# First chunk of the first expert in whole float32, batch 0 turned by transposes, and filler matmuls in TensorE's pauses

## The chip, the cores and the metric

One core of a Trainium2 chip runs the kernel. The metric is the time of an execution on the device in microseconds. Before the change three runs took 937.07, 938.40 and 940.15 us, so the median is 938.4 us.

## What is computed

An attention with two parts, a pooled one over means of four tokens and a local one over the nearest tokens, feeds two feed-forward layers, one after the other, for 2304 tokens of width 512.

```python
def _attn_ref(q, k, v):                      # 4 batches, 8 heads, 576 tokens, 64 wide
    q_d, k_d, v_d = (t.reshape(B, H, S // 4, 4, D).mean(axis=3) for t in (q, k, v))
    out_up = np.repeat(sm_attn(q_d, k_d, v_d), 4, axis=2)       # softmax attention, pooled
    mask = np.abs(pos[:, None] - pos[None, :]) < 4              # local attention
    scores = np.where(mask, scale * q @ k.T, -1e9)
    return out_up + softmax(scores) @ v
x = attention output as [2304, 512]
h = x @ w_in; x = np.where(h > 0, h, exp(min(h, 0)) - 1) @ w_out          # d_ff 2048
g = x @ w_gate; out = (g * sigmoid(g) * (x @ w_val)) @ w_o2               # d_ff 1536
```

The two weights of the first layer and the three of the second come as 64-bit floats; the kernel makes 32-bit floats of their bit patterns.

## The kernel before

**The planner.** The whole kernel is a list of tasks. `add(engine, cost, due, fn, reads, writes, ...)` records one; `Work.run` then plays the time out, with the costs that are written beside each task, and emits in each engine's program whatever ready task has the smallest due time. So the order of the instructions on each engine is settled ahead, and on the chip each engine runs its list in order and waits for what each entry needs. The capital names (`START`, `EAGER`, `PARTS`, ...) are due times and offsets of that list. `urge` gives everything that the first product needs a due time from the length of its chain. DMAs are issued from one queue, SP's. `fetched` models the loading of TensorE's own instructions, in blocks of 256; only some tasks state their number (`words`).

**Batch 0.** `add_first_batch` loads q and k in 16 DMAs, two heads and half the sequence each, 72 partitions with pieces of 1 KB, and turns each part by eight matmuls against `ident` (L734) into `qT` and `kT`; a copier (L352 on ACT, L354 on DVE) brings the result from its PSUM bank. `add_sums` pools four tokens (L620 on DVE, L625 and L626 on POOL). `add_pooled` does one pair of heads of the pooled attention: scores (L812), maxima (L819), exponentials (L825), weights (L835), their turning (L850), values (L866). `add_local` does one unit of 96 tokens of the local attention: scores (L640), softmax (L658 to L680), the spread into `bd` (L352), values (L709). Units 0 to 2 are the first chunk; units 3 to 5 come later, between its products. `add_split` adds both parts into `f` (L987), rounds the sum into `x[..., 0]` (L352 or L354) and puts the remainder in `x[..., 1]` (L998, POOL).

**Weights.** `add_weights` loads each block of 512 KB and makes words of it: `size` (L509, ACT), `rest` (L515 on ACT or L513 on DVE), `words` (L519, DVE). `add_weight_split` rounds a block (L352 or L356) and subtracts (L554, POOL), since the products are made of rounded parts, hi x hi, hi x lo and lo x hi, in `products` (L1010 to L1012).

**The first layer.** Chunks of 288 tokens run over 16 blocks f of the hidden width: `gemm1` (x to h), ELU on ACT and DVE, `gemm2` (g to the accumulators). `add_whole` does this for chunk 0. There gemm1 is twelve split products and needs the split of block ("in", f) and of x; gemm2 is already four plain float32 matmuls (L1044) with the unsplit block ("out", f). Chunks 1 to 4 use split blocks for both. The rest of the first layer and the second layer use a seven-product scheme.

**Start.** Seven bf16 matmuls of 512 columns (`warm_up`, L1692) run first; `clear` sets all of `qT` and `kT` to zero on POOL (L1696).

## Time and profile before

| | |
|---|---|
| median of three runs | 938.4 us |
| the profiled execution | 937.54 us |
| its span, from the first to the last instruction | 935.8 us |
| mean granted TensorE clock | 0.978 |
| TensorE busy | 913.0 us |
| DVE, ACT, POOL busy | 566.3, 523.1, 533.6 us |

The profile is one execution, recorded on the chip. Its views are the page with busy times, the busy time in chosen stretches, the engines' instructions in order of time, the groups of instructions by line, and the chain of waits that leads to the end. The granted clock is a share of full speed: 1.00 is 2.4 GHz, 0.50 is 1.2 GHz. A float32 matmul stands as two instructions; the record of a matmul is longer than the distance to the next one, as they overlap.

### The profile page before, as it was taken

To read this page: it belongs to the slowest core of one execution; us is meant where nothing else is said; L and a number is where in the kernel's file an instruction comes from. 1 tells how busy PE (TensorE), PEld (TensorE's weight loads), DVE (VectorE), ACT (ScalarE), POOL (GpSimd) and SP (SyncE) were. 2 spreads that over 40 slices of the span, in tenths; PEclk is the share of its full clock that TensorE was granted. 3 is DMA by queue.
4 is the path that set the end of the run, shared out by engine and by line. 5 is a ranking of instruction groups with operands and counts; after the bars stand their busy time and mean duration, and the time that the engine had idled before them with its cause. 6 is when DMAs were issued, how large, how long until landed. Compare 5 with 4: busy or idle time off the path is not lost.

```text
span 935.8 us, 19972 instructions
## 1 busy us (share of the span) xinstructions
PE 913.0 (98%) x7573; PEld 829.0 (89%) x7573; DVE 566.3 (61%) x937; ACT 523.1 (56%) x1125; POOL 533.6 (57%) x609
## 2 busy tenths in 40 slices
PE   8779999999999999999999999999999999999998
PEld 7568889999999999999999888887888887999998
DVE  2988777777677249444337385435434247896773
ACT  3988566454556457675665456555546435453441
POOL 6797956664665459489791408998899940000000
PEclk7589999999999999999999999999999999999999
DMA  6999445659745654565588613452554299854331
GB/s 172 309 270 276 82 125 126 139 178 315 132 114 152 189 186 140 163 204 195 187 296 326 247 61 124 169 191 91 210 181 183 104 350 308 273 170 135 127 113 46
DMA packets 194704, 172.12 MB, mean 184 GB/s; under 512 B 96176, under 2 KB 166192, under 8 KB 194608
## 3 DMA queue, kind: packets, MB, share of 16 engines
q1 hardware_dynamic: 194464, 170.58, 58.2%
q8 instruction: 60, 0.98, 0.4%
q14 instruction: 36, 0.29, 0.1%
q10 hardware_dynamic: 144, 0.26, 0.1%
HBM read 111.62 MB, written 59.18 MB: 183 GB/s over the span
## 4 chain that ended last, share of the span: by engine, by line
PE 91%; DMA 4%; DVE 2%; SPq 1%; ACT 1%; issue 1%; POOL 0%; DVEq 0%
PE bank L1010 28%; PE bank L1011 27%; PE bank L1012 27%; PE bank L1044 3%; PE bank L640 2%; PE bank L709 2%; DMA w<-in_v_dram 2%; DMA w<-in_moe_w_in_dram 1%; DMA w<-in_k_dram 1%; PE bank L915 1%; PE bank L909 1%; PE bank L962 1%; DVE xh L1191 1%; SPq L595 0%; DMA wd<-mid 0%
## 5 line engine op out<-in xcount | busy, mean ns | idle before, releaser
L1010 PE MATMUL bank<-xs,wu 128*128 128x512 f32 x336 | 133.4, 397 | 2.4 <-DVE blk L1223 2.0
L1012 PE MATMUL bank<-xs,wu 128*128 128x512 f32 x336 | 133.2, 396 | 0.0
L1011 PE MATMUL bank<-xs,wu 128*128 128x512 f32 x336 | 133.2, 396 | 0.0
L1010 PE MATMUL bank<-os,ys 128*128 128x256 f32 x378 | 107.2, 283 | 1.0 <-DVE o L1223 1.0
L1011 PE MATMUL bank<-os,ys 128*128 128x256 f32 x378 | 107.0, 283 | 0.0
L1012 PE MATMUL bank<-os,ys 128*128 128x256 f32 x378 | 106.9, 283 | 0.0
L1010 PE MATMUL bank<-x,w 128*128 128x288 f32 x320 | 100.2, 313 | 1.4 <-DVE e L1088 0.9
L1010 PE MATMUL bank<-g,w 128*128 128x288 f32 (+1 forms) x320 | 101.0, 316 | 0.0
L1223 DVE TENSOR_TENSOR blk<-bank,blk 128x512 f32<-128x512 f32 x72 | 49.5, 690 | 81.7 <-PE bank L1012 75.4
L1011 PE MATMUL bank<-g,w 128*128 128x288 f32 (+1 forms) x320 | 98.5, 308 | 0.0
L1012 PE MATMUL bank<-g,w 128*128 128x288 f32 (+1 forms) x320 | 98.3, 307 | 0.0
L1011 PE MATMUL bank<-x,w 128*128 128x288 f32 x320 | 95.3, 298 | 0.0
L1012 PE MATMUL bank<-x,w 128*128 128x288 f32 x320 | 94.9, 296 | 0.0
L1095 POOL TENSOR_TENSOR g<-e,g 128x288 fp32r<-128x288 f32 x64 | 57.2, 894 | 56.0 <-ACT g L352 44.7
L1220 ACT COPY blk<-bank 128x512 f32<-128x512 f32 x72 | 42.0, 585 | 72.9 <-PE bank L1012 66.0
L1010 PEld LDWEIGHTS bank<-xs,wu 128*128 128x128 f32 x336 | 63.3, 188 | 17.7 <-DVE blk L1223 2.9
L1012 PEld LDWEIGHTS bank<-xs,wu 128*128 128x128 f32 x336 | 63.3, 188 | 15.4
L1011 PEld LDWEIGHTS bank<-xs,wu 128*128 128x128 f32 x336 | 63.3, 188 | 14.0
L1010 PEld LDWEIGHTS bank<-os,ys 128*128 128x128 f32 x378 | 72.5, 192 | 1.6 <-DVE o L1223 1.4
L1011 PEld LDWEIGHTS bank<-os,ys 128*128 128x128 f32 x378 | 72.5, 192 | 0.1
L1012 PEld LDWEIGHTS bank<-os,ys 128*128 128x128 f32 x378 | 72.5, 192 | 0.0
L1191 POOL TENSOR_TENSOR wu<-s,wu 128x256 fp32r<-128x256 f32 x79 | 59.7, 783 | 18.5 <-ACT wu L1194 18.4
(213 smaller groups left out, 2525.3 us busy)
## 6 DMA issues: line engine op xcount, KB each, us to landing
yr<-yd SPq DMA_DIRECT2D x27, 512.0 KB
yd<-blk SPq DMA_DIRECT2D x24, 512.0 KB
os<-od SPq DMA_DIRECT2D x42, 256.0 KB
w<-in_moe_w_in_dram SPq DMA_DIRECT2D x16, 512.0 KB
w<-in_moe_w_out_dram SPq DMA_DIRECT2D x16, 512.0 KB
wp<-w SPq DMA_DIRECT2D x16, 512.0 KB
wu<-wp SPq DMA_DIRECT2D x16, 512.0 KB
u<-wd SPq DMA_DIRECT2D x32, 256.0 KB
```

The costliest lines, as they stand in the source:

```text
L640: nc.tensor.matmul(sc[j].t[s * QB:(s + 1) * QB, (u * NP + p) * QB:(u * NP + p + 1) * QB], parts["qT"][p].t[j * D:(j + 1) * D, a:a + QB], p ...
L709: nc.tensor.matmul(pvs[u].t[j * D:(j + 1) * D, p * U:(p + 1) * U], tvs[u].t[:, (2 * p + j) * D:(2 * p + j + 1) * D], bd.t[:, u, j * NP + p ...
L909: nc.tensor.matmul(sc[0].t[j * D:(j + 1) * D, 2 * G:3 * G], vs0.t[:, w, j], prT0.t[:, j, w], start=(w == 0), stop=(w == 1))
L915: nc.tensor.matmul(sc[j].t[:HALF, u * G:(u + 1) * G], t[:, 0, p, u * HALF:(u + 1) * HALF], t[:, 1, p], start=True, stop=True)
L1010: nc.tensor.matmul(ps, sh, mh, start=first, stop=False, skip_group_check=more)
L1011: nc.tensor.matmul(ps, sh, ml, start=False, stop=False, skip_group_check=more)
L1012: nc.tensor.matmul(ps, sl, mh, start=False, stop=last, skip_group_check=more)
L1044: nc.tensor.matmul(acc[0][i].t[:, :T1], wo.t[:, i * P:(i + 1) * P].bitcast(F32), ge(), start=f == 0, stop=f == NF1 - 1)
L1095: add("pool", 0.86, due - URGENT, lambda e=e, g=g: nc.gpsimd.tensor_tensor(out=g.t[:, 1], in0=e.t, in1=g.t[:, 0], op=ALU.subtract), reads= ...
L1191: return task(engines, n, due, lambda engine=engines[0]: two(engine).tensor_tensor(out=out(), in0=in0(), in1=in1(), op=op), reads, writes, ...
L1220: return add("act", ps_copy, when(m) - 20, lambda: nc.scalar.copy(d(i), ps.t[:, :w]), reads=[ps], writes=of(i))
L1223: return add("dve", ps_sum, when(m) - 20, lambda: nc.vector.tensor_tensor(out=d(i), in0=ps.t[:, :w], in1=d(i), op=ALU.add), reads=[ps], wr ...
```

## The change

- Chunk 0: gemm1 becomes four plain float32 matmuls on the unsplit block ("in", f) and on x as it is. `add_split` writes the sum into x directly for this chunk. The splits of ("in", f) are made later, for chunk 1, rounded by ACT alone, as those of ("out", f).
- Batch 0: q and k are loaded as eight parts of two heads with the whole sequence, six tokens to a partition, 96 partitions, two DMAs with pieces of 256 bytes each. Each part is turned by six transposes of 96 x 128 (both heads at once) into two banks. The rows of v for the pooled part come in one load for two, and token pairs are interleaved in the matmuls' access patterns. Local scores wait for all parts.
- TensorE's pauses: where the planner finds TensorE without a ready task, from the first turning to the first product, it emits a bf16 matmul that nobody reads, 32 x 64 or 128 x 512. The warm-up becomes 72 of the small ones. Bank 7 is kept for it.
- Every task of TensorE states or estimates its number of instructions; `fetched` uses it for all.
- `clear` covers only the margins. The value loads are tasks by piece, with their memsets apart. `add_weights` may put raw blocks in any slot once products run; `add_direct` uses a PSUM bank. ACT may scale the pooled weights. Most due times and several costs have new values.

```diff
         t.costs = {engine: cost} if isinstance(engine, str) else dict(zip(engine, cost))
+        t.words = words + 1 if words else int(self.RATE * t.costs.get("pe", 0.0)) + 1
...
                     if t is None:
+                        filled = engine == "pe" and self.filler and self.filler()
+                        if filled:
+                            free[engine] = now + self.fetched(2, now, filled)
+                            seq += 1
+                            heapq.heappush(events, (free[engine], seq, None))
...
-                    if t.words:
-                        cost = self.fetched(t, now, cost)
+                    if engine == "pe":
+                        cost = self.fetched(t.words, now, cost)
...
-        return banks.new(lambda: [4, 5] if late or begun else [6, 0, 1, 2, 3, 7])
+        return banks.new(lambda: [4, 5] if late or begun else [6, 0, 1, 2, 3])
...
-    WARM = 7
+    WARM = 72
+    SHORT = 435.62
...
-            raw, w, ps = w_raws.new(lambda: range(NW - 1, U1 - 1, -1)), whole(n), bank(4, 5)
+            raw, w, ps = w_raws.new(lambda: range(NW - 1, -1 if begun else U1 - 1, -1)), whole(n), bank(4, 5)
...
-        for k, (p, u, which) in enumerate((p, u, which) for p in range(NP) for u in range(2) for which in range(2)):
+        for k, (p, which) in enumerate((p, which) for p in range(NP) for which in range(2)):
             name, start = (("qT", 0), ("kT", PAD))[which]
-            t, dst, pt = rows[k], parts[name][p], att_bank()
-            cols = slice(start + u * UPC * U, start + (u + 1) * UPC * U)
-            add("sp", 0.5, FIRST + 0.5 * k, lambda t=t, p=p, u=u, name=name: nc.sync.dma_start(
-                out=t.t, in_=rows_of(name[0], 0, u, 2 * p, 2 * p + 2)), writes=[t], nbytes=HALF * 2048 * 1.2)
-
-            def turn(t=t, pt=pt):
-                for r in range(R):
...
-            add("pe", 0.56, FIRST + k - EAGER, turn, reads=[t], writes=[pt, dst], slack=SLACK, kind="small", after=ready[:1], words=32)
-            made[which, p, u] = add(COPIER, (0.41, 0.45), FIRST + k + 1, lambda engine, dst=dst, pt=pt, cols=cols: copy(
-                engine, dst.t[:, cols], pt.t[:, :UPC * U]), reads=[pt], writes=[dst], second=1)
+            t, dst = rows[k], parts[name][p]
+            full = dst.room.make(p)[:, start:start + S]
+
+            def load(t=t, p=p, name=name):
+                for j in range(2):
+                    nc.sync.dma_start(
+                        out=t.t.rearrange("g (r j d) -> g r j d", j=2, d=D)[:, :, j],
+                        in_=source[name[0]][0, 2 * p + j].rearrange("(g r) d -> g r d", r=SIX))
+
+            add("sp", 1.0, FIRST + 1.0 * k, load, writes=[t], nbytes=P * S * 4 * 1.35)
+            of = []
+            for u in range(2):
+                pt, to = att_bank(), full.rearrange("c (g r) -> c r g", r=SIX)[:, 3 * u:3 * u + 3]
+
+                def turn(t=t, pt=pt, u=u):
+                    turning.append(1)
+                    for r in range(3):
+                        nc.tensor.transpose(
+                            pt.t[:, r * S // SIX:(r + 1) * S // SIX], t.t[:, (3 * u + r) * P:(3 * u + r + 1) * P], ident[:S // SIX, :S // SIX])
+
+                add("pe", 0.3, FIRST + 2 * k + u - EAGER, turn, reads=[t], writes=[pt, dst], slack=SLACK, kind="small", after=ready[:1], words=6)
+                of.append(add(COPIER, (0.41, 0.46), FIRST + 2 * k + u + 1, lambda engine, to=to, pt=pt: copy(
+                    engine, to, pt.t[:, :S // 2].rearrange("c (r g) -> c r g", r=3)), reads=[pt], writes=[dst], second=1))
+            made[which, p] = of
             summed.setdefault((0, p), []).append(add_sums(
-                FIRST + k + 2, lambda dst=dst, cols=cols: dst.t[:, cols].rearrange("p (g r) -> p g r", r=R),
...
-        for u in range(2):
-            t = raws[u]
-            add("sp", 0.5, load_due, lambda u=u, t=t: nc.sync.dma_start(
-                out=t.t, in_=rows_of("v", b, u, 2 * p, 2 * p + 2)), writes=[t], nbytes=HALF * 2048 * 1.2)
-            rowed.append(add("pool", 1.18, due, lambda t=t: add_rows(t.t), reads=[t]))
...
+        add("sp", 0.5, load_due, lambda: nc.sync.dma_start(
+            out=raw.t, in_=rows8("v", b, 2 * p, 2 * p + 2)), writes=[raw], nbytes=HALF * 4096 * 1.15)
+        rowed.append(add("pool", 2.05, due, add_rows, reads=[raw]))
...
                     nc.tensor.matmul(
-                        sc[j].t[:HALF, u * G:(u + 1) * G], t[:, 0, p, u * HALF:(u + 1) * HALF], t[:, 1, p], start=True, stop=True)
-
-        add("pe", 0.9, due + 1 - EAGER, scores, words=16, holds=[qk], after=summed[b, p], writes=[*sc, mx, nm, su, pr], slack=SLACK, kind="small")
+                        sc[j].t[:HALF, u * G:(u + 1) * G], t[:, 0, p].rearrange("c (g u) -> c g u", u=2)[:, :, u], t[:, 1, p], start=True, stop=True)
...
         add("dve", 1.35, due + 2 - FREE, maxima, reads=sc, writes=[mx, nm])
         add("act", 1.14, due + 3 - FREE, weigh, reads=[*sc, nm], writes=[pr, su])
         add("dve", 0.6, due + 4, norm, reads=[su], writes=[su])
-        add(EITHER, (1.01, 1.14), due + 4.3, weight, reads=[pr, su], writes=[pr])
+        add(("act", *EITHER), (1.28, 1.01, 1.14), due + 4.3, weight, reads=[pr, su], writes=[pr], second=1)
...
-                            pws[j].t[:HALF, w * G + u * HALF:w * G + (u + 1) * HALF],
-                            pr.t[:, j, u, w * HALF:(w + 1) * HALF], ident[:HALF, :HALF])
+                            pws[j].t[:HALF, w * G:(w + 1) * G].rearrange("k (g u) -> k g u", u=2)[:, :, u],
+                            pr.t[:, j, u].rearrange("q (k w) -> q k w", w=2)[:, :, w], ident[:HALF, :HALF])
...
-        add(EITHER, (0.77, 1.05) if n >= UPC else (1.0, 0.9), due, lambda engine: both(engine, f()), reads=[xf, xdT[b]], writes=[xf])
+        if c == 0:
+            return add(EITHER, (1.0, 0.9), due, lambda engine: both(engine, x.t[:, :, 0, cols].bitcast(F32)), reads=[xf, xdT[b]], writes=[x])
+        add(EITHER, (0.77, 1.05), due, lambda engine: both(engine, f()), reads=[xf, xdT[b]], writes=[xf])
...
-        add_weight_split(("in", f), due - EARLY, w_slots.new(lambda: range(NW)), ("pool", "act"), PREFER)
-        wi, wo, x = wt["in", f], ww["out", f], xt[0]
+        wi, wo, x = ww["in", f], ww["out", f], xt[0]
...
-                cs = slice(i * P, (i + 1) * P)
-                products(h.t[:, :T1], (wi.t[:, 0, cs], wi.t[:, 1, cs]), (x.t[:, i, 0], x.t[:, i, 1]), i == 0, i == NP - 1)
+                nc.tensor.matmul(
+                    h.t[:, :T1], wi.t[:, i * P:(i + 1) * P].bitcast(F32), x.t[:, i, 0].bitcast(F32), start=i == 0, stop=i == NP - 1)
...
-        inner[:] = [add("pe", 12 * 0.1325, due - STEP, gemm1, reads=[wi, x], writes=[h], after=inner)]
+        inner[:] = [add("pe", 1.73, due - STEP, gemm1, words=16, reads=[wi, x], writes=[h], after=inner)]
...
-        last[0] = [add("pe", 1.93, due + STEP, gemm2, reads=[wo, g], writes=acc[0], after=last.get(0, ()), slack=1.0)]
-        split_last = [add_weight_split(("out", f), time1(NF1 + f + 1) + PARTS, w_slots.new(split_places), COPIER[:1])]
+        last[0] = [add("pe", 1.73, due + STEP, gemm2, words=16, reads=[wo, g], writes=acc[0], after=last.get(0, ()), slack=1.0)]
+        split_last = [add_weight_split(("in", f), time1(NF1 + f) + PARTSI, w_slots.new(split_places), COPIER[:1]),
+                      add_weight_split(("out", f), time1(NF1 + f + 1) + PARTS, w_slots.new(split_places), COPIER[:1])]
...
-        raw = gens.new([P, 1024], I32, name="r")
+        raw, ps = gens.new([P, 1024], I32, name="r"), banks.new(lambda: range(8) if ending else range(4, 8))
...
         def warm_up():
             for _ in range(WARM):
-                nc.tensor.matmul(warm, zeros[:, :P], zeros, start=True, stop=True)
+                nc.tensor.matmul(warm[:QB, :64], zeros[:, :QB], zeros[:, :64], start=True, stop=True)
+
+        def fill():
+            if begun or not turning:
+                return 0.0
+            if work.words < SHORT and (work.border - work.words > 16 or work.arrives < work.now):
+                nc.tensor.matmul(warm[:QB, :64], ident.bitcast(BF16)[:, :QB], ident.bitcast(BF16)[:, :64], start=True, stop=True)
+                return work.FILLS[1]
+            some = ident.bitcast(BF16).rearrange("p (o n) -> p o n", o=1).to_broadcast([P, 2, 2 * P])
+            nc.tensor.matmul(warm.rearrange("p (o n) -> p o n", o=2), ident.bitcast(BF16)[:, :P], some, start=True, stop=True)
+            return work.FILLS[0]
+
...
         def clear():
-            for name in ("qT", "kT"):
-                nc.gpsimd.memset(turned[name], 0.0)
...
+            nc.gpsimd.memset(q[:, :, S:], 0.0)
+            nc.gpsimd.memset(k[:, :, :PAD], 0.0)
+            nc.gpsimd.memset(k[:, :, PAD + S:], 0.0)
...
-            add("sp", 2.0, LATER + n if late else VALUES + n, lambda n=n: load_values(0, n * U, vals[n].t), writes=[vals[n]], nbytes=P * H * D * 4 * 3.1)
-            turned_by = [t for (which, p, u), t in made.items() if u == (late or 0) or (which and (n == UPC - 1 or n == UPC))]
+            for s, edge, load in value_pieces(0, n * U):
+                due = (LATER if late else VALUES) + n
+                clean = [add("pool", 0.52, -900.0 + s, lambda n=n, s=s: nc.gpsimd.memset(vals[n].t[s * QB:(s + 1) * QB], 0.0), writes=[vals[n]])] if edge else ()
+                add("sp", 0.5, due, lambda n=n, load=load: load(vals[n].t), writes=[vals[n]], after=clean, nbytes=QB * H * D * 4 * 1.8)
+            turned_by = [t for ts in made.values() for t in ts]
...
-        whole = [w_slots.new(lambda: range(U1)) for _ in range(NF1)]
...
+        whole = [w_slots.new(lambda: range(NW if begun else U1)) for _ in range(NF1)]
...
```

## Rows read from the trace of the kernel before

**Rows 1.** The page: busy us (share of the span) and instructions by engine.

```profile
PE 913.0 (98%) x7573; PEld 829.0 (89%) x7573; DVE 566.3 (61%) x937; ACT 523.1 (56%) x1125; POOL 533.6 (57%) x609
```

**Rows 2.** Busy time by stage: stretch, length, engines, granted clock, DMA share, GB/s.

```profile
32.00:46.00 14.00, 12.82 (x112) 11.18 (x112) 13.35 (x32) 13.32 (x33) 8.54 (x11) 0.51 1.08 355
...
52.60:56.00 3.40, 3.40 (x15) 3.18 (x14) 2.54 (x6) 2.26 (x4) 3.40 (x4) 0.51 1.07 219
...
60.00:124.00 64.00, 63.84 (x598) 54.04 (x598) 51.99 (x101) 43.87 (x96) 50.94 (x55) 1.00 0.78 195
124.00:936.00 812.00, 803.45 (x6308) 735.97 (x6294) 475.17 (x745) 439.15 (x922) 438.69 (x489) 1.00 0.55 179
```

**Rows 3.** The chain of waits, 0 to 130 us: start, us, what.

```profile
9.70 5.50 DMA w<-in_k_dram
```

**Rows 4.** TensorE in order of time: start, us, line, tiles, count, [idle before].

```profile
1.19 3.17 PE L1692 MATMUL warm<-bd 128*128 128x512 bf16 x7 [1.19 <-DVE bd L1687]
...
6.15 13.05 PE L734 MATMUL bank<-ident,w 72*64 72x72 f32 x224 [0.47 <-DMA w<-in_q_dram]
...
24.41 0.91 PE L812 MATMUL bank<-sums 64*72 64x144 f32 x8 [1.70 <-DVE w L658]
...
32.08 1.17 PE L850 MATMUL bank<-ident,w 72*72 72x72 f32 x8 [3.38 <-POOL w L835]
...
42.31 3.24 PE L709 MATMUL bank<-bd,w 128*64 128x96 f32 x32
...
52.56 0.61 PE L1010 MATMUL bank<-x,w 128*128 128x288 f32 x1
```

**Rows 5.** ACT, DVE and POOL in order of time, before the first product.

```profile
39.90 1.45 ACT L352 COPY bd<-w 32x192 f32<-32x192 f32 x4
...
46.61 0.47 ACT L352 COPY f<-bank 128x384 f32<-128x384 f32 x1
...
46.96 0.54 DVE L987 TENSOR_TENSOR f<-f,xdT 128x384 f32<-128x384 f32 x1
...
48.33 0.98 POOL L987 TENSOR_TENSOR f<-f,xdT 128x384 f32<-128x384 f32 x1
```

**Rows 6.** The chain of waits at clock 1.00: start, us, what, count.

```profile
70.94 0.76 PE bank L640 x49
...
75.45 0.13 PE bank L1010
...
77.04 1.94 PE bank L1044 x8
...
82.50 1.47 PE bank L709 x32
...
126.51 0.50 PE bank L962 x8
...
130.26 0.65 PE bank L909 x8
```

**Rows 7.** Groups by line from 20 to 53 us: count | busy, mean ns | idle.

```profile
L825 ACT ACTIVATE w<-bank,nm 72x144 f32<-72x144 f32 x16 | 5.8, 373 | 1.8 <-DVE nm L820 1.8
...
L835 POOL TENSOR_TENSOR w<-w,su 72x576 f32<-72x576 f32 x3 | 3.4, 1138 | 0.0
...
L819 DVE TENSOR_REDUCE mx<-bank 72x2 f32<-72x288 f32 x8 | 3.3, 443 | 0.5 <-PE bank L812 0.5
```

**Rows 8.** Busy time of four short stretches, columns as in rows 2.

```profile
4.00:12.00 8.00, 7.44 (x141) 6.77 (x142) 0.45 (x1) 3.19 (x8) 2.22 (x5) 0.76 0.80 205
...
10.00:12.00 2.00, 2.00 (x38) 2.00 (x36) 0.00 (x0) 0.84 (x3) 0.00 (x0) 0.50 0.86 208
...
22.00:24.00 2.00, 0.71 (x66) 0.60 (x64) 1.97 (x6) 0.52 (x2) 1.84 (x5) 1.00 0.39 86
...
90.00:96.00 6.00, 6.00 (x41) 5.58 (x40) 4.82 (x9) 5.12 (x12) 5.26 (x6) 1.00 0.95 136
```

**Rows 9.** Groups by line from 53 to 125 us, the rounding of weights on ACT.

```profile
L352 ACT CAST w<-w 128x512 fp32r<-128x512 f32 x15 | 8.8, 615 | 4.7 <-POOL w L554 2.5 <-POOL half L625 1.5 <-PE bank L1044 0.6
```

211 lines of the change are left out of this document (115 added, 96 removed).

## The prediction, made before the changed kernel was run

> **What bounds the kernel now.** Three views, in this order. First the page's busy times: TensorE is busy 913.0 of 935.8 us, apart from its own weight loading nothing is above 61%, so only two things can shorten this kernel: less TensorE work, or less time in which TensorE idles or runs at its lower clock [rows 1]. Second the busy time by stage: from 124 us to the end TensorE idles 8.55 us of 812, from 60 to 124 us 0.16 of 64, and the granted clock is 1.00, the 2.4 GHz level [rows 2]. Nearly all the rest lies before 56 us, where the clock is about 0.51, the 1.2 GHz level, in the rows of 32 to 46 and of 52.6 to 56 us [rows 2]. So the question is when the first chunk's products begin (52.56 us, [rows 4]) and what TensorE must do from there. After that moment the kernel is a queue of TensorE work: a microsecond earlier is a microsecond off the end, and a microsecond of added TensorE work comes straight on top.
>
> Third the start itself, in order of time. The last q/k load is issued at 9.70 us and lands at 15.2 [rows 3]. TensorE turns these rows into qT and kT without a pause from 6.15 to 19.20, 224 small matmuls at 58 ns each [rows 4] at a clock of 0.50 [rows 8]. The softmax of four pooled heads and three local units follows; from 32.08 to 45.55 us TensorE works through 112 instructions (32 turn the pooled weights, 32 are pooled values, 48 local values) at 0.51 [rows 2, 4]. Then x is finished: the last local output is copied at 47.08, added to the pooled part by 49.31, then rounded and its remainder subtracted, and the first product starts at 52.56 [rows 4, 5].
>
> **The change, part by part.**
>
> *x whole.* The sum now goes straight into x; the copy and the remainder fall away for three units. After the copy at 47.08 there is one addition: 0.54 us on DVE, 0.98 on POOL [rows 5]. x is ready at 47.6 to 48.1 where the first product started at 52.56: 4.5 to 5.0 us, of which I take 4.5.
>
> *Products of the first chunk in float32.* The second product of this chunk has that form already: four matmuls, eight instructions, 1.94 us. The first one takes from 75.45 to 77.04, that is 1.59 us for twelve [rows 6]. It becomes 1.94, so 16 x 0.35 = 5.6 us are added, in a stretch where TensorE idles 0.16 us of 64 [rows 2]. Nothing covers that: it counts whole.
>
> *Splits of the input weights behind.* They no longer stand before the first product, but the first split was done before x was, so I take nothing for it beyond the first part. All 32 roundings go to ACT now, which made 15 of them from 53 to 125 us [rows 9], the others mostly POOL. That is a debt, below.
>
> *Turning by transposes.* 256 instructions become 48 transposes of 96 columns. Eight transposes of 72 columns take 0.50 us at clock 1.00 [rows 6] and 1.17 at 0.5 [rows 4], so one of 96 takes 83 to 195 ns, and only the last six (0.5 to 1.2 us) can lie behind the last landing, instead of 4.0 us. Against it, q and k come in pieces of 256 bytes instead of 1 KB. Pieces of 1 KB ran at 205 GB/s with the DMA engines 0.80 busy, 256 GB/s per full share; the v loads with pieces of 256 bytes at 86 with 0.39, 220 per full share; pieces of 128 bytes at 136 with 0.95, 143 [rows 8]. 2.36 MB at a share of 0.80 thus take 11.5, 13.4 or 20.7 us: 0 to 9.2 us more. I take 1.9, the row with the same size of piece. The turning then ends at 17.6 to 18.3 instead of 19.2; I take 1.2 us.
>
> The Trainium skill ("DMA: Bandwidth & Descriptors", Why small descriptors are slow) gives a descriptor of 256 bytes 11 bus cycles where 8 move data. By that an estimate for these loads is 11.5 x (11/8)/(35/32) = 14.5 us, 3.0 more than now instead of my 1.9; its specifications call for 512 bytes or more, which speaks against this part of the change.
>
> *Pooled heads during the loads.* TensorE had no room for pooled scores before 19.2 us. With the turning cheaper it has, and heads 0 to 2 can run while later heads still load. Per head ACT spends 4 x 0.37 us, DVE 2 x 0.44, POOL 1.14 [rows 7]; three heads are up to 4.4 us on ACT, which is busy 13.32 of 14 us from 32 to 46 [rows 2]. Bounds 0 and 4.4; I take 3, as ACT was nearly full there. The local scores wait longer instead: for all eight parts, not for one half. Behind them on TensorE stand the pooled scores, whose parts come earlier, so I add nothing.
>
> *Pauses filled.* If the clock is up from 32 us on, the 112 instructions take 4 x 0.50 (turning), 4 x 0.65 (pooled values), 1.5 x 1.47 (local values) = 6.8 us [rows 6] instead of 13.5. But ACT releases the last local values only at 41.35 [rows 5]; from there 0.7 (their matmuls) and 0.47 (the copy) lead to 42.5, not 47.08: 4.6 us. I take 4, between 0 and 6.7. Also the first products ran at half speed: 15 in 3.40 us [rows 2], which take 15 x 0.13 = 2.0 at 1.00 [rows 6], so 1.4 us more after the start. A filler in front of a ready instruction delays it by at most its own length; the seven matmuls of the warm-up, of the same form, took 3.17 us [rows 4], 0.45 each. The two long pauses, 1.70 us before 24.41 and 3.38 before 32.08 [rows 4], end in work of the chain: 0 to 0.9 us, I take 0.5.
>
> *The rest.* v rows in one load for two, values by pieces with the memsets as tasks of their own, a shorter clear: POOL and the SP queue have them before the transposes end, and the chain doesn't wait for them; zero, and at most 2 us. One local score set that stood before 52.56 falls behind the start: 0.8 us [rows 6]. New due times order everything after 124 us anew; TensorE idles 8.55 us there, so 4 us either way; zero. The direct weights' use of a PSUM bank lies in that bound too.
>
> *Sum.* The start: 4.5 + 4 + 1.2 + 3 - 0.5 = 12.2 us earlier, at 40.4. After it: + 5.6 - 1.4 + 0.8 = + 5.0. Together - 7.2. The profiled execution took 937.54 us (span 935.8), so 930.3; the median of the runs is 0.9 higher, 938.4, so 931.2.
>
> **Rivals.**
>
> *All bounds at their good end.* 5.0 + 6.7 + 2.5 + 4.4 = 18.6 us, a start at 34, with the same + 5.0 after it: about 925. For it: DVE and ACT were mostly idle before 19 us. Against it: the same engines must still convert weights.
>
> *The fills don't bring the clock.* TensorE issued matmuls without a pause from 10 to 12 us at 0.50, and the clock was 1.00 from 22 to 24 us, where it was busy 0.71 of 2.00 [rows 8]: what the fillers do to it no row shows. If nothing, the 4 and the 1.4 us are lost: 931.2 + 5.4 = 936.6, no difference that can be measured.
>
> *The loads are slow.* If pieces of 256 bytes go like those of 128, the last landing is 9.2 us later and not 1.9: 938.5, no difference.
>
> *ACT becomes the bound in the first chunk: slower.* ACT gets the 32 roundings of 0.615 us [rows 9], 19.7 us, beside weights, ELU and late attention, and 12 us less of head start. The exponentials of each step stand behind them in ACT's queue, and TensorE waits for these. Each rounding that stands in front of an awaited exponential costs up to its 0.615 us; from 18 of 32 (11 us) on the kernel is slower than before, with 24 it takes 931.2 + 14.8 = 946. Against it: ACT was busy 43.87 of 64 us there [rows 2].
>
> **How the numbers follow.** Chances: forecast 0.50 (927 to 935), good end 0.14, clock 0.13, loads 0.10, ACT 0.13. A measurement here can tell about 0.3% from no change, that is 935.6 and 941.2. Faster: 0.50 + 0.14 and 0.07 of the clock and load cases, 0.71; the rest of those two within, 0.16; slower 0.13. The predicted time is that of the forecast, 931; the range from 922, inside the good end, to 940, over the cases without difference, leaves out ACT and a little below.
>
> **What would show it.** Right: first product at 37 to 44 us; a clock of 1.00 in most rows from 20 us on; the first product's four matmuls at 1.94 us; TensorE without idle time in the first chunk. Wrong: last landing of k after 20 us; fillers directly ahead of waiting work; TensorE waiting on g behind ACT's roundings; idle time after 124 us well over 8.55 us.

## The result, and the profile after

The changed kernel takes 944.0 us (median; 943.5 to 947.23) beside 938.4 before: a ratio of 1.0063, interval 1.0040 to 1.0086. It is 0.6% slower, where 931 was predicted. The profiled execution of after took 947.23 us (span 945.5). That is 9.7 us more than the profiled execution of before (937.54), and 3.2 more than the median of after itself.

The first view is again the busy time by stage, with the columns of [rows 2] (engines PE, PEld, DVE, ACT, POOL); the second stretch begins at the first product of after.

```profile
32.00:46.00 14.00, 11.73 (x151) 6.95 (x149) 9.99 (x30) 10.70 (x32) 4.92 (x6) 0.76 1.01 358
50.90:56.00 5.10, 4.34 (x18) 3.04 (x17) 3.95 (x8) 4.16 (x8) 2.32 (x4) 1.00 1.02 230
60.00:124.00 64.00, 64.00 (x392) 49.59 (x390) 45.68 (x98) 49.60 (x108) 35.06 (x41) 1.00 0.81 208
124.00:946.00 822.00, 808.84 (x6360) 740.42 (x6358) 468.33 (x763) 437.30 (x918) 445.63 (x501) 1.00 0.56 177
```

The clock did rise where the fills stand, 0.76 instead of 0.51 from 32 to 46 us, and 1.00 at the first products. But from 124 us on TensorE idles 13.2 us (822.00 - 808.84) instead of 8.55, and POOL does 15.9 us less from 60 to 124 (35.06 instead of 50.94). Nine of its roundings (5.9 us) went to ACT. Of the 32 subtractions of the splits, before makes 24 (31.5 us) from 60 to 124 and none from 124 to 215; after makes 15 (19.0 us) and then 16 (21.1 us). So half of them lie behind 124 us now.

TensorE in order of time (start, us, line, operation, count, [idle before]) shows the second thing: the first product comes at 50.88 us, 1.7 us earlier than before [rows 4], and not 12.2. The run of the form alone (below), which has the same list as before up to there, came at 53.40, so about half of this gain is within the spread of single executions.

```profile
24.60 0.34 PE L663 MATMUL bank<-kT,qT 64*32 64x32 f32 x29
27.90 1.23 PE L663 MATMUL bank<-kT,qT 64*32 64x32 f32 x99 [2.96 <-issue]
...
45.49 2.12 PE L1740 MATMUL warm<-ident 128*128 128x512 bf16 x9
47.53 0.88 PE L732 MATMUL bank<-bd,w 128*64 128x96 f32 x16
48.35 0.39 PE L1740 MATMUL warm<-ident 128*128 128x512 bf16 x1
48.67 0.76 PE L663 MATMUL bank<-kT,qT 64*32 64x32 f32 x64
49.35 1.69 PE L1740 MATMUL warm<-ident 128*128 128x512 bf16 x7
50.88 2.10 PE L1075 MATMUL bank<-x,w 128*128 128x288 f32 x8
53.74 0.48 PE L1075 MATMUL bank<-x,w 128*128 128x288 f32 x1 [0.76 <-DVE w L529]
```

In the middle of the local scores (L663, which is L640 in the kernel before) TensorE stands 2.96 us and waits for nothing that the profile shows ("issue"). Nine fills (L1740) stand ahead of the last local values (L732), seven ahead of the first product.

The other queues, in order of time, show what else grew in the start:

```profile
17.03 11.26 SPq L610 DMA_DIRECT2D w<-in_v_dram  x13
28.34 0.74 SPq L479 DMA_DIRECT2D w<-in_moe_w_in_dram  x1
...
34.98 0.43 DVE L523 TENSOR_SCALAR w<-w 128x512 uint32<-128x512 uint32 x1 [1.52 <-DMA w<-in_moe_w_out_dram]
...
48.46 0.56 DVE L363 COPY f<-bank 128x384 f32<-128x384 f32 x1 [1.63 <-PE bank L732]
49.26 1.00 DVE L1022 TENSOR_TENSOR x<-f,xdT 128x384 f32<-128x384 f32 x1
```

The thirteen value loads take SP's queue 11.26 us (6.88 before), the first weight is issued at 28.34 (25.59 before), and DVE, with the softmax queued behind, waits for a weight. The end of the chain is as short as foreseen: copy, one addition, product.

Behind the first chunk one more pair of engines matters: DVE and POOL, and TensorE at the end of it.

```profile
136.69 5.02 POOL L564 TENSOR_TENSOR w<-w 128x512 fp32r<-128x512 f32 x4
...
137.46 4.28 DVE L979 TENSOR_SCALAR su<-su 72x4 f32<-72x4 f32 x1
141.77 0.17 DVE L980 RECIPROCAL su<-su 72x4 f32<-72x4 f32 x1
...
158.95 3.44 DVE L689 TENSOR_TENSOR sm<-sm,st 128x512 f32<-128x512 f32 x1
...
162.91 0.44 PE L997 MATMUL bank<-ident,pr 72*72 72x72 f32 x4 [1.50 <-DVE f L363]
```

An operation on 72x4 numbers lasts 4.28 us on DVE; it ends as POOL ends four subtractions of left-behind splits in a row. The reciprocal behind it, of the same size, takes 0.17.

**Where the time lies.** A chunk ends here where the first store of its output is issued. In us, of one profiled execution each (those of the experiments are told of below):

| kernel | first product | chunk 0 ends | chunk 1 lasts | ratio to before, with interval |
|---|---|---|---|---|
| before | 52.56 | 122.12 | 72.8 | 1 |
| after | 50.88 | 123.54 | 78.4 | 1.0063 (1.0040 to 1.0086) |
| no fills | 46.90 | 126.04 | 74.8 | 1.0072 (1.0053 to 1.0091) |
| few instructions | 50.30 | 123.65 | 74.5 | 1.0061 (1.0038 to 1.0083) |
| long pieces | 50.66 | 123.31 | 74.4 | 1.0063 (1.0042 to 1.0083) |
| long pieces, few instructions | 47.92 | 120.57 | 74.7 | 1.0033 (1.0019 to 1.0048) |
| long pieces, no fills | 43.66 | 118.40 | 75.7 | 1.0009 (0.9992 to 1.0025) |
| the same, port-free forms | 43.63 | 118.36 | 71.8 | 0.9971 (0.9956 to 0.9987) |
| the same, 13 fills | 44.39 | 117.13 | 73.1 | 0.9985 (0.9964 to 1.0005) |
| after, port-free forms | 50.17 | 123.76 | 71.8 | 1.0016 (1.0002 to 1.0030) |

Single executions differ: the first product of the kernel before came at 52.56, and in the kernel before with port-free forms, whose median is the same, at 53.72; there chunk 0 ended at 124.00 instead of 122.12. So a difference of 1 to 2 us between two rows means little by itself.

Chunk 1's 78.4 us in the profile of after contain a stretch of 8 us at a clock of 0.57 (164 to 172 us, right behind the wait at 162.91); 8 x 0.43 = 3.4 us is about what that execution lies above the median. Of the rows below it only long pieces without fills shows something like it, 0.59 from 158 to 162 us, behind the same kind of wait.

Chunk 1 alone can't be compared between before and the kernels derived from after, as their plans put different work of TensorE into it. In the same columns as above, but with TensorE's busy time alone, chunks 1 and 2 of before, and below them those of the run with port-free forms:

```profile
122.12:194.93 72.81, 72.47 (x1094) 1.00 0.53 124
194.93:263.32 68.39, 68.39 (x818) 1.00 0.80 227
...
118.36:190.20 71.84, 70.87 (x969) 1.00 0.42 87
190.20:260.84 70.64, 70.44 (x944) 1.00 0.81 220
```

Both chunks together take 141.2 us in before, 149.5 in after, 145.7 with few instructions, 146.5 with long pieces and no fills, 142.5 with these and port-free forms, and 142.2 in after with port-free forms.

### The profile page after: what moved, and what is told of

It reads as the page before. It is cut to its first block, busy times and chain, and to the rows that moved or that the text cites. A ratio compares the mean times of both kernels' runs of the same rounds, so it can differ in the third digit from the quotient of the medians.

```text
span 945.5 us, 19725 instructions
## 1 busy us (share of the span) xinstructions
PE 923.7 (98%) x7485; PEld 825.1 (87%) x7485; DVE 550.1 (58%) x945; ACT 524.5 (55%) x1128; POOL 508.9 (54%) x589
## 4 chain that ended last, share of the span: by engine, by line
PE 85%; DVE 5%; DMA 4%; SPq 4%; issue 1%; ACT 1%; POOL 0%; DVEq 0%; ACTq 0%
PE bank L1047 25%; PE bank L1049 24%; PE bank L1048 24%; PE bank L1080 3%; PE bank L1075 3%; DMA w<-in_moe_w_in_dram 1%; PE bank L663 1%; PE bank L732 1%; SPq L754 1%; DMA wd<-mid 1%; DVE xh L1228 1%; SPq L610 1%; DMA w<-in_v_dram 1%; SPq L484 1%; PE bank L944 1%
## 5 line engine op out<-in xcount | busy, mean ns | idle before, releaser
L1132 POOL TENSOR_TENSOR g<-e,g 128x288 fp32r<-128x288 f32 x64 | 54.7, 855 | 62.9 <-ACT g L361 44.6
L1047 PE MATMUL bank<-x,w 128*128 128x288 f32 x256 | 78.4, 306 | 2.6 <-DVE e L1125 2.6
L1048 PE MATMUL bank<-x,w 128*128 128x288 f32 x256 | 76.0, 297 | 0.0
L1049 PE MATMUL bank<-x,w 128*128 128x288 f32 x256 | 75.9, 297 | 0.0
L1228 POOL TENSOR_TENSOR wu<-s,wu 128x256 fp32r<-128x256 f32 x79 | 59.4, 778 | 13.2 <-ACT wu L1231 12.8
```

What stands on the lines that cost most here:

```text
L1047: nc.tensor.matmul(ps, sh, mh, start=first, stop=False, skip_group_check=more)
L1048: nc.tensor.matmul(ps, sh, ml, start=False, stop=False, skip_group_check=more)
L1049: nc.tensor.matmul(ps, sl, mh, start=False, stop=last, skip_group_check=more)
L1132: add("pool", 0.86, due - URGENT, lambda e=e, g=g: nc.gpsimd.tensor_tensor(out=g.t[:, 1], in0=e.t, in1=g.t[:, 0], op=ALU.subtract), reads= ...
L1228: return task(engines, n, due, lambda engine=engines[0]: two(engine).tensor_tensor(out=out(), in0=in0(), in1=in1(), op=op), reads, writes, ...
```

## The experiments

The kernels derived from after keep its order on every engine: the planner plans as before, and only what is emitted differs.

### Without the fills

```diff
-                nc.tensor.matmul(warm[:QB, :64], ident.bitcast(BF16)[:, :QB], ident.bitcast(BF16)[:, :64], start=True, stop=True)
                 return work.FILLS[1]
...
-            nc.tensor.matmul(warm.rearrange("p (o n) -> p o n", o=2), ident.bitcast(BF16)[:, :P], some, start=True, stop=True)
             return work.FILLS[0]
```

> Order of every engine as in the changed kernel, but the 119 filling matmuls between turning and the first product are not issued (the 72 of the warm-up stay). Three theories of why the first product came at 50.88 us. (I) The filling matmuls are themselves the trouble: they use up TensorE's instructions (it stood 2.96 us in the middle of the local scores at its 700th instruction) and stand ahead of ready work (0.9 us before the last local values, 0.5 before the first product). Then the stop at 24.9 us is gone, the first product comes at 46 to 47 and the median falls by about 4 us, to 940. (C) The fills hold TensorE's clock up and that is worth as much as it costs: clock 0.50 from about 8 us on, turning 2 us later, first product at 50 to 52, median 944 to 946. (L) The loads and the queue of DMAs decide: first product within 1.5 us of 50.88 whatever TensorE does, median 943 to 945.

Measured: 945.53 us. TensorE in order of time:

```profile
28.64 0.34 PE L663 MATMUL bank<-kT,qT 64*32 64x32 f32 x9 [1.80 <-issue]
...
46.90 4.18 PE L1075 MATMUL bank<-x,w 128*128 128x288 f32 x8 [0.81 <-DVE x L1022]
53.29 3.25 PE L1075 MATMUL bank<-x,w 128*128 128x288 f32 x6 [2.21 <-DVE w L529]
```

The first product comes 4.0 us earlier without the fills, at the lower clock: the fills took more from the chain to x than the clock gave it (I is right on the start). But 4.18 us for eight instructions that took 2.10 in after, and 2.21 of waiting for the second weight, give it all back: chunk 0 ends later than in after (C is right on the sum). The stop in the scores is there too, 90 scores later in the program than in after, but at the same number of TensorE's recorded instructions (687 matmuls and weight loads from the start in both).

### Fewer instructions

```diff
-            for _ in range(WARM):
-                nc.tensor.matmul(warm[:QB, :64], zeros[:, :QB], zeros[:, :64], start=True, stop=True)
+            for _ in range(7):
+                nc.tensor.matmul(warm, zeros[:, :P], zeros, start=True, stop=True)
...
-                nc.tensor.matmul(warm[:QB, :64], ident.bitcast(BF16)[:, :QB], ident.bitcast(BF16)[:, :64], start=True, stop=True)
                 return work.FILLS[1]
```

> As the changed kernel, but with 276 fewer instructions of TensorE before its stop: the 73 short filling matmuls are not issued, and the warm-up is again seven matmuls of 512 columns instead of 72 of 64. The 46 long fills stay. (I) The stop of 2.96 us comes from TensorE's instructions arriving late: it goes, or comes some 276 instructions later where TensorE waits for others anyway; first product at 47.5 to 49, median 941 to 942.5. (C) If only the long fills matter for the clock, it stays at 1.00 in 16 to 27 us as before. (L) The loads decide: first product at 50 to 51.5, median 943 to 945, whether the stop goes or not.

Measured: 944.25 us, first product at 50.30. The stop in the scores is gone, and another has come, of the same length:

```profile
32.28 0.66 ACT L525 ACTIVATE w<-w 128x512 int32<-128x512 uint32 x1 [2.20 <-DMA w<-in_moe_w_in_dram]
...
33.75 0.72 PE L901 MATMUL bank<-w 72*64 72x144 f32 x8 [3.12 <-issue]
```

ACT waits 2.20 us for the first weight; behind it in its queue stand the exponentials of the fourth pooled head, and the pooled values (L901) start just behind the second of these, which frees a PSUM bank. That it is this bank is inferred from the times, in this run and in after (L901 at 34.48): 0.8 us behind the end of ACT's L525 in both. So I failed in its time and its median, and L's came true, with this wait in the place of the stop. C held: the clock is 1.00 from 16 to 27 us. That the stop went because there were fewer instructions is not shown: after with port-free forms (below) has all of them and no such stop either.

### Long pieces

```diff
-                for j in range(2):
-                    nc.sync.dma_start(
-                        out=t.t.rearrange("g (r j d) -> g r j d", j=2, d=D)[:, :, j],
-                        in_=source[name[0]][0, 2 * p + j].rearrange("(g r) d -> g r d", r=SIX))
+                nc.sync.dma_start(
+                    out=t.t.rearrange("g (j x) -> g j x", j=2),
+                    in_=source[name[0]][0, 2 * p:2 * p + 2].rearrange("j (g r) d -> g j (r d)", r=SIX))
...
-                        nc.tensor.transpose(
-                            pt.t[:, r * S // SIX:(r + 1) * S // SIX], t.t[:, (3 * u + r) * P:(3 * u + r + 1) * P], ident[:S // SIX, :S // SIX])
+                        for j in range(2):
+                            nc.tensor.matmul(
+                                pt.t[j * D:(j + 1) * D, r * S // SIX:(r + 1) * S // SIX],
+                                t.t[:, (6 * j + 3 * u + r) * D:(6 * j + 3 * u + r + 1) * D], ident[:S // SIX, :S // SIX], start=True, stop=True)
...
-            for _ in range(WARM):
-                nc.tensor.matmul(warm[:QB, :64], zeros[:, :QB], zeros[:, :64], start=True, stop=True)
+            for k in range(24):
+                if k < 7:
+                    nc.tensor.matmul(warm, zeros[:, :P], zeros, start=True, stop=True)
+                else:
+                    nc.tensor.matmul(warm[:QB, :64], zeros[:, :QB], zeros[:, :64], start=True, stop=True)
```

> As the changed kernel, but q and k are loaded in pieces of 1536 bytes, one DMA for two heads instead of two with pieces of 256 bytes; each transpose of 96x128 becomes two matmuls of 96x64, and the warm-up has 24 matmuls of the same total time instead of 72, so that TensorE has issued as many instructions when the turning ends. (L) The loads and their queue decide: 16 issues of 0.65 us become 8 of about 0.4, so the value loads and the weights behind them are issued some 5 us earlier, the last turning ends at 14 to 15.5 instead of 17.7, first product at 46 to 47.5, median 939 to 941. (I) TensorE's instructions decide: the stop stays at the same count of instructions and only grows as TensorE reaches it earlier; first product at 49 to 51, median 942 to 944.5.

Measured: 944.83 us. SP's queue and TensorE in order of time:

```profile
21.40 0.45 SPq L479 DMA_DIRECT2D w<-in_moe_w_in_dram  x1
...
28.28 0.90 PE L663 MATMUL bank<-kT,qT 64*32 64x32 f32 x66 [2.78 <-issue]
...
50.66 4.33 PE L1076 MATMUL bank<-x,w 128*128 128x288 f32 x16
```

The weights are issued 6.9 us earlier, and the first product gains 0.2 us. L alone is refuted. A stop of 2.78 us remains, though at 945 recorded instructions and not at 687; I's first product came true, its median missed by 0.3 us. Each of the two edits alone gains next to nothing: another wait of about 3 us takes the place of the one that is gone.

### Both together

> Long pieces for q and k and few instructions of TensorE together: 1536-byte pieces in one DMA for two heads, two matmuls of 96x64 for each transpose, no short fills, a warm-up of seven long matmuls. Each of the two alone left the first product where it was (50.66 and 50.30 us instead of 50.88): with the early loads TensorE still stood 2.8 us for its instructions, with few instructions it stood 3.1 us behind a bank that ACT freed late, as ACT waited 2.2 us for the first weight. (B) If each covers the other, both together free the start: no stop over 1 us in the local scores nor before the pooled values, first product at 46.5 to 48, median 940 to 941.5. (O) If a third thing sets it (the order of DVE's queue, the fills ahead of the last local values), it stays at 49.5 to 50.7 and the median at 943 to 945.

The diffs are those of the last two, with the warm-up of the fewer instructions. Measured: 942.09 us, first product at 47.92, 3.0 us earlier than in after. So they do cover each other (B), but not wholly: the median misses B's range by 0.6 us, as here the weights are issued at 24.14 only and ACT still waits for the first, and with the same effect:

```profile
29.16 0.66 ACT L525 ACTIVATE w<-w 128x512 int32<-128x512 uint32 x1 [1.94 <-DMA w<-in_moe_w_in_dram]
...
30.64 1.24 PE L902 MATMUL bank<-w 72*64 72x144 f32 x8 [2.26 <-issue]
```

### Long pieces and no fills

> Long pieces for q and k, and none of the filling matmuls issued; a warm-up of 24. Without the fills alone the first product came at 46.90, but then TensorE ran its first products at 0.50 and waited 2.2 us for the second weight's words, and the chunk ended no earlier. (B) With the weights loaded 7 us earlier that wait is gone: first product at 44.5 to 46.5, the chunk of 32 products ends at 120 to 122.5 instead of 123.5 to 126.0, median 940 to 942. (C) If the low clock takes back what the earlier start gives, the chunk ends at 123 or later and the median is 943 to 945.

The diffs are those of the long pieces, with its warm-up of 24, and of the run without fills. Measured: 938.28 us, as before. The first product comes at 43.66, 7.2 us earlier than in after, and chunk 0 ends 5.1 us earlier: better than B's range on both counts and in the median, and 3.7 us earlier than before there. The low clock takes its part, 9.09 us for 24 instructions that take 3 x 1.94 = 5.8 at 1.00 [rows 6]:

```profile
43.66 9.09 PE L1076 MATMUL bank<-x,w 128*128 128x288 f32 x24 [1.37 <-DVE x L1023]
```

The 3.7 us don't reach the end: chunks 1 and 2 together take 146.5 us against 141.2, 5.3 more, and later stages give a little back.

### The first product's form alone, in the kernel before

```diff
-                cs = slice(i * P, (i + 1) * P)
-                products(h.t[:, :T1], (wi.t[:, 0, cs], wi.t[:, 1, cs]), (x.t[:, i, 0], x.t[:, i, 1]), i == 0, i == NP - 1)
+                nc.tensor.matmul(
+                    h.t[:, :T1], wi.t[:, 0, i * P:(i + 1) * P].bitcast(F32), x.t[:, i, 0].bitcast(F32), start=i == 0, stop=i == NP - 1)
```

> The kernel before in its own order, with one thing changed: the first product of chunk 0 is four float32 matmuls on the rounded weights and the rounded x, instead of twelve split products (the low parts are left out of that product). By the step of the prediction, 16 x 0.35 us more, all of it on the path: median 938.5 + 5.6 = 944. (H) If part of it is hidden (by TensorE's waits, or as other work then needs no pause), less: 940 to 942. (M) If float32 products also bring TensorE's waits or the clock elsewhere, over 946.

Measured: 943.61 us, ratio 1.0060 (1.0045 to 1.0075), that is 4.2 to 7.0 us. The term of 5.6 us was right within that interval, and no part of it is seen to be hidden.

### The float32 part alone, planned anew

```diff
+        if c == 0:
+            return add(EITHER, (1.0, 0.9), due, lambda engine: both(engine, x.t[:, :, 0, cols].bitcast(F32)), reads=[xf, xdT[b]], writes=[x])
...
-        inner[:] = [add("pe", 12 * 0.1325, due - STEP, gemm1, reads=[wi, x], writes=[h], after=inner)]
+        inner[:] = [add("pe", 1.93, due - STEP, gemm1, reads=[wi, x], writes=[h], after=inner)]
...
-        split_last = [add_weight_split(("out", f), time1(NF1 + f + 1) + PARTS, w_slots.new(split_places), COPIER[:1])]
+        split_last = [add_weight_split(("in", f), time1(NF1 + f) + PARTS, w_slots.new(split_places), COPIER[:1]),
+                      add_weight_split(("out", f), time1(NF1 + f + 1) + PARTS, w_slots.new(split_places), COPIER[:1])]
...
```

> The kernel before with one part of the change alone: the first product of chunk 0 in whole float32 on the unsplit weights, the sum straight into x, the splits of these weights made later by ACT and POOL. Turning, loads, due times and warm-up as before, no fills. By the steps of the prediction: first product 4.5 us earlier, at about 48, then 5.6 us more in the chunk, median 938.4 - 4.5 + 5.6 = 939.5. (D) If the splits that are left behind are a debt, TensorE stands idle or slow by some us more between 124 and 250 us, as it did in the changed kernel (4.5 us idle, and 7 us at clock 0.50): median 943 or more. (N) If it is only the changed order that makes that loss, idle time after 124 us stays at 8 to 9 us.

Measured: 956.69 us, beyond all of it. The planner made another order of it, with the first product at 58.53; neither D nor N can be read from it. It shows the hold of DVE at its worst (the addition takes 0.54 us in [rows 5]):

```profile
52.36 6.02 DVE L987 TENSOR_TENSOR x<-f,xdT 128x384 f32<-128x384 f32 x1
...
52.63 1.69 POOL L987 TENSOR_TENSOR x<-f,xdT 128x384 f32<-128x384 f32 x2
54.27 3.70 POOL L554 TENSOR_TENSOR w<-w 128x512 fp32r<-128x512 f32 x3
...
58.53 3.76 PE L1040 MATMUL bank<-x,w 128*128 128x288 f32 x8 [8.53 <-DVE x L987]
```

### POOL's subtractions twice

```diff
-        return add("pool", 1.32, due - 1, lambda: nc.gpsimd.tensor_tensor(
-            out=w.t[:, 1], in0=u.t.bitcast(F32), in1=w.t[:, 0], op=ALU.subtract), reads=[u, w], writes=[w])
...
+        def lower():
+            for _ in range(1 + bool(begun)):
+                nc.gpsimd.tensor_tensor(out=w.t[:, 1], in0=u.t.bitcast(F32), in1=w.t[:, 0], op=ALU.subtract)
...
+        return add("pool", 1.32, due - 1, lower, reads=[u, w], writes=[w])
```

> The changed kernel in its order, but POOL makes the subtraction of every weight split of the first layer from chunk 0 on twice (the same result). (D) If these subtractions are a debt that holds DVE up (its instructions lasted 4.28 us instead of 0.22 and 3.44 instead of 0.68 while POOL worked without a pause), then POOL's 19.8 us between 126 and 208 us become 40, DVE's stretched instructions grow, TensorE's idle time in chunk 1 grows from 2.8 us to over 6, and the median rises by 4 us or more, to 948 or later. (N) If POOL's work there lies beside the path, the median moves by less than 1.5 us.

Measured: 973.61 us, much more than D asked for, but not by D's mechanism. From chunk 0 to the end of chunk 1 the group has 60 instructions of 79.0 us in sum; DVE's longest held operation is 2.64 us, and TensorE waits for POOL's own queue (who waited for whom, 135 to 227 us: us in total, times, longest):

```profile
PE bank L1052 <- POOL g L1136: 10.4, 3, 5.8
```

So POOL has no room for twice the work; what the hold costs, it doesn't tell.

### Port-free forms of two small operations

```diff
-            nc.vector.tensor_scalar_add(sums_of(), sums_of(), 1e-9)
...
-                nc.vector.tensor_scalar(out=su.t, in0=su.t, scalar1=1e-9, scalar2=float(R), op0=ALU.add, op1=ALU.mult)
-                nc.vector.reciprocal(out=su.t, in_=su.t)
+                nc.vector.reduce_sum(out=mx.t.rearrange("p j u -> p (j u)"), in_=su.t.rearrange("p j (u o) -> p (j u) o", o=1).to_broadcast([HALF, 4, R]), axis=X)
+                nc.vector.reciprocal(out=su.t.rearrange("p j u -> p (j u)"), in_=mx.t.rearrange("p j u -> p (j u)"))
...
```

On long pieces and no fills:

> As the run with long pieces and no fills (938.3 us), in the same order on every engine, but two small operations of DVE take forms that were never held while POOL worked: the 72x4 scaling of the pooled sums (0.17 us alone, up to 4.29 us held, 8.6 us in sum between 100 and 420 us) becomes a reduction over four equal columns, and the addition of 1e-9 to the local sums (0.17 alone, up to 1.0) is left out, as these sums are at least 1. (D) If POOL's left-behind subtractions cost through DVE being held, TensorE's idle time in chunk 1 falls from 2.8 to 1.5 us or less, as the larger local subtraction that was held 3.4 us stays, and the median falls to 936.0 to 937.5. (N) If what is held lies beside the path, or the hold only moves to the next operation with two inputs, 938 to 939.

On the changed kernel itself, and on the kernel before:

> The changed kernel itself, same order on every engine, with the two port-free forms of DVE's small operations alone (the pooled scaling as a reduction, the 1e-9 left out). (D) On the kernel with long pieces and no fills they gave 2.2 us, chunk 1 going from 75.7 to 71.8 us: here chunk 1 goes from 78.4 (74.4 in its undisturbed relatives) to 72 or less and the median from 944 to 941 to 942.5, the start staying at about 50.9. (N) If that gain hung on the other order of events there: 943.5 to 944.5.

> The kernel before, same order on every engine, with the same two forms. (D) Its DVE was held far less in these operations (0.74 us at most, 2.3 and 1.1 in sum) and TensorE did not stand once between 122 and 263 us, so there is nothing to gain: 938 to 939, no difference over 0.2%. (N) If the forms gain by themselves, by DVE's shorter work: 937 or less, and then the gain seen in the other kernels is not that of the change's debt.

Measured: 936.06, 941.08 and 938.54 us. Chunk 1 goes from 75.7 to 71.8 us in the first and to 71.8 in the second; the median falls by 2.2 and 2.9 us (by the ratios 3.6 and 4.4); the kernel before gains nothing (0.9999, 0.9990 to 1.0008). Which of the two forms gives the gain isn't separated. The medians are D's in all three, and N's in none. The groups by line from 100 to 420 us in the first, and who waited there in chunk 1 of the second (100 to 300 us):

```profile
L979 DVE TENSOR_REDUCE mx<-su 72x4 f32<-72x16 f32 x12 | 2.0, 166 | 0.4
```

```profile
PE bank L731 <- issue: 0.9, 1, 0.9
```

The scaling as a reduction is never held, 166 ns in the mean of twelve, and the waits of 1.3 and 1.50 us in chunk 1 have shrunk to one of 0.9. The hold itself went on to the next operation with two inputs, but there it costs less (TensorE idles 1.0 us in chunk 1 instead of 2.9):

```profile
132.69 4.47 DVE L983 TENSOR_TENSOR pr<-pr,su 72x576 f32<-72x576 f32 x1
```

The first of the three beats both kernels, by 0.3% the kernel before.

The second also bears on the stop in the scores. Up to there TensorE has the same list as in after, and all 128 scores run through; the stop comes later, again behind ACT's wait for the first weight, and the first product stays at 50.17:

```profile
25.70 1.34 PE L663 MATMUL bank<-kT,qT 64*32 64x32 f32 x128
...
33.06 1.03 PE L900 MATMUL bank<-w 72*64 72x144 f32 x8 [3.10 <-issue]
```

### Thirteen fills

The diff to the run with long pieces, no fills and port-free forms; the long fill itself is issued again behind these lines:

```diff
...
+            consecutive, seen[0] = work.now - seen[0] < 0.35, work.now
+            if consecutive:
+                return work.FILLS[0]
...
```

> As the run before it in this list, but with one long fill (two instructions) at the head of each pause in which the changed kernel had a row of them: 13 fills instead of 119. (F) If few fills are enough for the clock, the first product comes at 44 to 45.5 (43.7 without fills, 47.9 with all long ones) and the first products run at 1.00 instead of 0.50, which took 3.3 us more: chunk 0 ends at 116 to 117.5 instead of 118.4, median 935 to 936.5. (C) If the clock stays at 0.50 until the products themselves raise it, the fills only add their length: chunk 0 ends at 118.5 to 119.5, median 937.5 to 939.

Measured: 937.69 us. The first product comes at 44.39 and runs at 1.00:

```profile
44.39 2.18 PE L1075 MATMUL bank<-x,w 128*128 128x288 f32 x8 [0.30 <-DVE x L1022]
```

Chunk 0 ends at 117.13, as F expected, 1.2 us earlier than without fills; the first product and the end of chunk 0 are F's, the median is C's (936.06 without fills), and the intervals of the two overlap. Whether a few fills pay stays open.

## Why the prediction was wrong

*What bounds the kernel*: right up to the end of chunk 0, where TensorE's work decides and it idles 0.76 us. Behind that, "a microsecond earlier is a microsecond off the end" did not hold: long pieces without fills end chunk 0 3.7 us earlier than before and take the same time in the median.

*Products in float32, + 5.6*: right; 5.3 by the run with that form alone (4.2 to 7.0). *Clock at the first products, - 1.4*: right in after (1.00 from 50.9 to 56 us).

*x whole, 4.5*: the mechanism is right, the size a little large. From the end of the last copy (49.02) to the first product (50.88) are 1.9 us instead of 5.5, so 3.6 gained. Of what is left, x was done at 50.26 and the product came 0.6 us later, behind seven fills; without fills it followed x by 0.15.

*Turning, 1.2*: right, the last transpose ends at 17.8 us instead of 19.2. But the same step put zero on SP's queue. The sixteen loads with short pieces occupy it to 12.2 us instead of 10.0, and what it issues behind them, values and weights, came later: the first weight by 2.75 us.

The Trainium skill ("DMA: Bandwidth & Descriptors", Why small descriptors are slow) puts more than the pure data time on each short piece. The trace agrees: from 8 to 12 us they move 205 GB/s at a share of 1.24; the pieces of 1536 bytes moved 249 to 285 from 6 to 10 us in five kernels, at 1.07 to 1.09. Single executions differ here: in after with port-free forms the same short pieces moved 214 at 0.98.

*Pauses filled, 4 less 0.5*: this is the step that failed. It took the lower clock for the limit of the chain and priced a fill at no more than its own length at two places. The clock came, but it gave less than the fills took: without fills, and at 0.50, the first product came 4.0 us earlier (46.90), and with long pieces 4.3 us earlier (43.66 against 47.92 with the long fills and a warm-up of fewer instructions). Even at 0.50 TensorE still waited for others in that run, 4.8 us in five waits between 28 and 43.7 us, as here:

```profile
31.54 1.15 PE L886 MATMUL bank<-ident,w 72*72 72x72 f32 x8 [1.23 <-ACT w L361]
```

The fills stand in TensorE's queue wherever the plan had seen a pause, and on the chip work was ready behind them: ACT had the last local weights in place at 46.57, and their values (L732) started at 47.53, behind nine fills. That was one of the prediction's own signs of being wrong. What the fills and the short warm-up add to the number of TensorE's instructions (146 and 144) may cost as well, by the stops that stand in the last section, but the runs don't settle that.

*Pooled heads, 3*: three heads did run during the loads, but the fourth's scores came at 30.55 us, behind the stop in the local scores; no run separates its worth.

*Splits behind, nothing*: wrong. It was called a debt and looked for on ACT (the rival of 946 us). It lies on POOL and DVE: the subtractions that POOL made in chunk 0 come in rows in chunk 1 and hold DVE. Two forms of small operations cost 2.9 us of the median there, and nothing in the kernel before. The rival's end was near the result, its mechanism was not: TensorE did not wait for ACT's exponentials behind roundings.

The Trainium skill ("SBUF — State Buffer", Who interferes with whom) speaks of this hold: DVE and GpSimd share a pair of ports, and the one that has it excludes the other. The trace agrees that they exclude each other (4.28 us for 0.17), but it shows the hold over four of POOL's instructions, where the page gives it for one. The prediction did not weigh that rule.

*The rest*: order and idle time behind 124 us were put at zero within 4 us. The hold isn't all that came there. From the store of chunk 3 to the first of chunk 4 the kernel before takes 54.1 us, after 56.5, after with port-free forms 56.9, and long pieces with port-free forms 58.7. TensorE's wait for DVE's e, an operand of the ELU, is part of it (us in total, times, longest; first in before, 329.4 to 383.5 us, then in long pieces with port-free forms, 326.8 to 385.5):

```profile
PE bank L1010 <- DVE e L1088: 0.9, 3, 0.5
...
PE bank L1047 <- DVE e L1125: 3.0, 3, 1.8
```

No run tells why. The port-free kernels lose part of their gain there; the rest of the kernel behind it is 1.3 to 3.2 us shorter than before in the kernels derived from after.

*The sum*: of 12.8 us between forecast and result 10.5 lie at the start (12.2 forecast, 1.7 had). Chunk 0 took 3.1 us more than before from its first product on, where 5.0 were forecast, so about 4.2 us lie behind it. The hold accounts for 2.9 of these; the rest is open, and of the size of the spread between executions. Without the fill term the forecast start is 52.56 - (12.2 - 3.5) = 43.9; long pieces without fills came at 43.66. The rival in which the fills bring nothing stood at 936.6; without fills, with long pieces and with the hold shortened the kernel takes 936.06. Both are agreements of sums, not proof of each term.

## What to carry over

Work that is moved out of the way lands in another engine's row: read who shares a port or a queue with it where it lands. Before a fill or a clock is priced, ask where the chain waits for TensorE at all and what stands ready behind the fill. Where two delays overlap, removing either shows nothing, so remove both before calling one harmless. And a microsecond won early is followed to the end before it is counted.

## What the runs showed of the hardware

- DVE's `TENSOR_SCALAR` on 72x4 and its `TENSOR_TENSOR` on two SBUF tensors were held while POOL worked without a pause, up to 4.28, 4.47 and 6.02 us; `RECIPROCAL` and `TENSOR_REDUCE` of the same 72x4 stayed at 0.17 us.
- TensorE stood 2.96, 1.80 and 2.78 us in the middle of runs of small matmuls, waiting for nothing that the profile shows, behind 687, 687 and 945 of its recorded instructions (after, no fills, long pieces). Shorter stops of this kind came behind 942 and 1187 in others (0.90 and 0.74 us). The places lie about 250 apart, and the instruction queue moved 59 packets (0.97 MB) in the whole of after, for 14970 recorded instructions of TensorE: one for 254, if all are TensorE's. In after one of them moved at the beginning of the stop (25.0 to 25.5 us: packets, MB, share):

```profile
q8 instruction: 59, 0.97, 0.4%
...
q8 instruction: 1, 0.02, 16.3%
```

- The number of instructions alone doesn't make such a stop. After with port-free forms has the same ones there and ran through; in it the packet moved from 20.5 to 21.0 us, 4.5 us earlier. That the stop is a wait for the packet is inferred, and what sets the time of the packet is not shown.
- In the re-planned kernel the granted clock was 1.00 from 2 to 50 us, and yet the turning by small matmuls ran no faster than at 0.50 in [rows 4, 8]: 61 ns each against 58. Why is not shown.

```profile
4.29 15.63 PE L734 MATMUL bank<-ident,w 72*64 72x72 f32 x256
```
